# A fused attention and feed-forward kernel: its first two groups become two chunks of one batch each, with two neighbouring tokens per partition, and the order of the program is written anew

## The chip, the core and the metric

The kernel runs on one core of a Trainium2 chip. The metric is device time in microseconds (us); the median of three runs of the kernel before is 174.61 us (174.01 to 174.85). The core's engines are named as the profile names them: PE (matrix products; PEld is its load of weights), DVE, ACT and POOL (element-wise work), SP (it only issues DMAs here).

## The reference

Four batches of 768 tokens, 8 heads of 48. First a linear attention with a decaying state per head, then a feed-forward block on all 3072 tokens:

```
for t in range(S):
    cur = einsum('bhd,bhe->bhde', u * kt, vt)
    y[:, :, t] = einsum('bhd,bhde->bhe', rt, state + cur)
    state = w * state + einsum('bhd,bhe->bhde', kt, vt)
h = x @ w_in                 # x: y as [3072, 384]; w_in [384, 2048]
g = where(h >= 1, h, where(h <= -1, 0, (h + 1)**2 / 4))
out = g @ w_out              # w_out [2048, 384]
```

## The kernel before

Tokens are cut into chunks of 128. A unit is one chunk of one batch; a **group** is two units, worked on together, and there are 12 groups. Group g covers chunk g // 2 of the batches 0 and 1 (g even) or 2 and 3 (g odd). So the groups 0 and 1 hold chunk 0 of all four batches, and no state enters them. Units are numbered n = 2g + j.

Within a chunk the recurrence is done as matrix products. The names of the steps are those of the word list `ORDER`, each of which calls the function `do_<name>`:

- `ln`, `bw`, `bu`, `wq`: the logarithm of w, laid over all partitions by a float32 matmul with a row of ones (tile lwp, L207), the same for u (tile up, L211), and per column (tile wp, L233). `WupS`, `WdnS`, `Wup`, `Wdn` make from lwp the tables of powers of w, on ACT.
- `LR`, `LK`, `LV`: DMA loads of r, k and v (tiles Ri, Ki, Vi), issued on SP's queue. In the groups 0 and 1 each is in two halves, one for each unit, of 192 KB; a piece of memory that lies together is one token of one head, 48 floats or 192 bytes.
- `Rs`, `Ks`: r and k times the tables, to bfloat16. `TR`, `TK` turn them by PE, `cR`, `cK` copy them out of PSUM (tile TT). Later groups are turned by DMA (`RT`, `KT`).
- `A`: products of k and r of the chunk (L370, eight matmuls for a unit, 48 rows of weights each). `AT`: the causal mask on DVE (L384; 128x512 here, two for a unit).
- `KU`, `RKU`, `us`, `B`: the part of the token itself, u k r v. `V`: cast of v (ACT).
- `Y` (L432, L438): A times v, and r times the state from the second chunk on. `y`: sum with B, on DVE.
- `X`, `xc`: y turned by PE and copied; later groups by a DMA transpose, `xcg` (L467).
- `Sp`, `Tm`, `decay`, `sbf`: the new state.
- `m` (L475): one of four blocks of h of a group, 12 matmuls. `r`, `s`, `g` make the activation from it: L486 and L495 on ACT, L498 on DVE. `M` (L512): a quarter of the second product for one unit, four matmuls, one for each f. `og`, `stg`: copy and store.
- `Z`: matmuls on a tile of zeros, with which PE fills waiting time.

The recording is by hand: every engine runs its own instructions in the order of `ORDER`, and a program waits only where data, a buffer or a PSUM bank asks for it. The letter behind `=` names the engine, the digits behind `/` PSUM banks or pairs of banks; while the groups 0 and 1 are in their attention part some banks are used singly (`bank`), else in four pairs (`pair`), which m, M, T, A, Y, Sp and X share. A step that asks for a pair waits until the pair's last reader is through. The weights w_in and w_out come by three DMAs each from POOL's queue (`WI`, `WO`), which cast to bfloat16; the third of either has the blocks 2 and 3.

Of the kernel before, what the change touches and what calls it, by code (L numbers as in the profile page):

```python
# [25 lines left out]
TK0/0 Wup/1 Rs0.0=V TR0/3 LK1.1 cK0=A WupS KU0.1=G KU0.0=V RKU0.0=G cR0=A KU1.0=G LV0.1 Rs0.1=V Z2 TR1/1 A0/03 LV1.0
LV1.1 WI0 WI1 WI2 us0.0 cR1=A TK1/1 cK1=A AT0.1 Z4 A1/13 Rs1.0=V LR2.0 LR2.1 Rs1.1=V V0.1 AT1.0 V0.0 Z9 TR3/1 B0.0=G
AT1.1 RKU0.1=V wE AT0.0 wC=A us0.1 Z7 Y1/3 TR2/0 B0.1=G Y0/2 y0 y1 cR2=A RKU1.0=G Z8 X0/2 Z4 TK2/3 X1/0 Ks1.1=G xc0=A
Sp1/2 cK2=A xc1=A Z7 TK3/3 cK3=A Tm1 A2/20 m0.0/0 cR3=V us1.0 AT2.1 AT2.0 r0.0=A A3/31 AT3.1 KU1.1=G RKU1.1=G m0.1/1
V1.0 s0.0=A B1.0=G Sp2/2 AT3.0 us1.1 r0.1=A Tm2 Y2/3 y2 g0.0 V1.1 X2/0 LK2.0 Y3/1 B1.1=G s0.1=A LK2.1 Sp0/2 Sp3/3  # L30
xc2=V LK3 y3 WO0 WO1 m0.3/0 r0.3=A s0.3=A g0.1 X3/1 Tm0 xc3=V m0.2/1 LR3 LV2.0 Tm3 m1.1/2 g0.3 r1.1=V m1.0/3 m1.2/0
Ks2=G r0.2=A s0.2=A g0.2 sbf2=A s1.1=A r1.0=A s1.0=A sbf3=A g1.1 m1.3/1 r1.2=V WO2 KU2=G LV2.1 M0.00/2 M0.10 M0.11
M0.01 g1.0 M1.00/3 M1.10 M1.11 M1.01 Rs2=G s1.2=A g1.2 T5/0 RKU2=G LK4 r1.3=A s1.3=A g1.3 T4/1 LV3 Ks3=G M0.02 M0.03
LR4 us2 c5=V A5/0 KU3=G Rs3=G c4=V A4/1 AT5 sbf1=A M1.02 M0.12 M0.13 AT4 T6/0 sbf0=A V2 Y4/1 Y5 B2=G og0=A T7/2 c6=A
# [40 lines left out]
def kernel(  # L75
# [52 lines left out]
    nc.scalar.dma_start(out=u_row, in_=u.rearrange("(o h) d -> o (h d)", o=1))
# [5 lines left out]
    nc.vector.memset(idle, 0.0)
# [78 lines left out]
    def do_Wup(e, b):  # L213
        t = tiles["up_t"] = pair(b[0], F32, "up_t")[:, 0, :DM]
        nc.scalar.activation(t, flat(tiles["lwp"]), AF.Exp, scale=up_col)

    def do_Wdn(e, b):
        t = tiles["dn_t"] = bank(b[0], [P, DM], F32, "dn_t")
        nc.scalar.activation(t, flat(tiles["lwp"]), AF.Exp, scale=dn_col)
# [391 lines left out]
```

## Time and profile before

| | us |
|---|---|
| median of three runs | 174.61 |
| span of the profiled execution | 172.6 |
| PE busy | 164.4 |
| DVE busy | 130.6 |
| ACT busy | 129.9 |
| POOL busy | 117.4 |

The profile gives the span of its one execution, from the first to the last instruction; 2.0 us lie between it and the median of the timed runs. The span falls into a start, in which the groups 0 and 1 go through attention and PE waits and fills (up to about 27 us), a long middle in which PE is busy without a break but for a short one near 74 us, and an end of some 3 us after PE's last matmul. In the timeline's rows the numbers are start and length, then engine, line, operation, output<-input, form and count; a bracket tells how long the engine had been idle before and what ended that.

### The profile page before, as it was taken

Reading aid. Unit: us, or ns where it says so; the run is one execution under the profiler, and the core shown is the slowest. Engines: PE = TensorE matmul, PEld = TensorE weight load, DVE = VectorE, ACT = ScalarE, POOL = GpSimd, SP = SyncE. Lnnn points to the kernel's source line nnn. Section 1 sums busy time; section 2 is a strip of 40 time slices with the busy share of each in tenths; the row PEclk is TensorE's granted clock in tenths of the full one; section 3 lists DMA queues with packets and bytes.
Section 4 is the critical chain, followed back from the end, with each engine's and each line's share of the span. In section 5 each row is a group of like instructions: output and inputs, shape, how many; then the busy total and the mean of one; then the engine's idle time right before and its main releaser. Section 6 shows DMA issues by size and latency. Waiting matters only on the chain.

```text
span 172.6 us, 4051 instructions
## 1 busy us (share of the span) xinstructions
PE 164.4 (95%) x1674; PEld 132.9 (77%) x1674; DVE 130.6 (76%) x150; ACT 129.9 (75%) x150; POOL 117.4 (68%) x86
## 2 busy tenths in 40 slices
PE   7989968999999999989999999999999999999991
PEld 5769868966889777588787797696897787888871
DVE  4578698988687688859789779885889959873752
ACT  4355698991699899189979879689695896988940
POOL 3496744998689949999999998999568804300000
PEclk9999999999999999999999999999999999999999
DMA  6999999998996999999999997998999025140022
GB/s 114 194 184 179 199 187 180 228 210 174 206 191 99 206 184 168 194 199 145 196 312 210 182 220 163 223 182 155 297 170 267 4 52 145 37 104 0 8 91 91
DMA packets 103751, 28.26 MB, mean 164 GB/s; under 512 B 98866, under 2 KB 102836, under 8 KB 103732
## 3 DMA queue, kind: packets, MB, share of 16 engines
q1 hardware_dynamic: 101824, 24.75, 79.9%
q0 software_dynamic: 1760, 3.15, 9.8%
q8 instruction: 13, 0.21, 0.6%
q10 hardware_dynamic: 148, 0.10, 0.2%
q14 instruction: 6, 0.05, 0.1%
HBM read 20.45 MB, written 4.72 MB: 146 GB/s over the span
## 4 chain that ended last, share of the span: by engine, by line
PE 87%; ACT 4%; DMA 2%; DVE 2%; issue 1%; POOL 0%; ACTq 0%; DVEq 0%
PE hp L475 35%; PE op L512 34%; PE A L370 4%; PE Y L438 3%; DMA xT<-y 2%; PE Y L432 2%; PE Sp L405 2%; PE z L566 2%; ACT pt L486 1%; PE T L330 1%; ACT TT L112 1%; PE lwp L207 1%; PE wp L233 1%; PE TR L330 1%; PE TK L330 1%
## 5 line engine op out<-in xcount | busy, mean ns | idle before, releaser
L475 PE MATMUL hp<-xT,w_in 128*128 128x256 bf16 x576 | 69.1, 273 | 1.3 <-DMA xT<-y 0.8
L512 PE MATMUL op<-w_out,g 128*128 128x384 bf16 (+1 forms) x400 | 68.4, 320 | 0.0
L498 DVE SCALAR_TENSOR_TENSOR g<-sq,hp 128x1024 bf16<-128x1024 bf16 x48 | 57.9, 1215 | 13.2 <-ACT sq L495 13.2
L475 PEld LDWEIGHTS <-w_in 128*128 128x128 bf16 x576 | 61.9, 114 | 4.6 <-issue 1.6
L486 ACT ACTIVATE pt<-hp 128x1024 f32<-128x1024 f32 x46 | 46.9, 1021 | 13.7 <-PE hp L475 13.7
L512 PEld LDWEIGHTS <-g 128*128 128x128 bf16 x400 | 37.5, 98 | 20.4
L495 ACT ACTIVATE sq<-pt 128x1024 bf16<-128x1024 f32 x46 | 48.3, 1057 | 1.2
L379 DVE TENSOR_TENSOR AT<-A,umask 128x1024 bf16<-128x1024 f32 x20 | 23.7, 1220 | 5.2 <-PE A L370 5.2
L282 POOL TENSOR_TENSOR Ks<-Ki,Wdn 128x768 bf16<-128x768 f32 (+1 forms) x12 | 20.3, 1689 | 8.5 <-ACT Wdn L225 3.4
L313 POOL TENSOR_TENSOR V<-Vb,diag 128x768 f32<-128x768 bf16 (+1 forms) x14 | 18.1, 1291 | 9.8 <-DVE diag L304 4.4
L282 POOL TENSOR_TENSOR RKU<-Ri,KU 128x768 f32<-128x768 f32 (+1 forms) x13 | 21.2, 1630 | 1.1 <-DVE KU L282 0.7
L282 POOL TENSOR_TENSOR KU<-Ki,u_sb 128x768 f32<-128x768 f32 (+1 forms) x13 | 21.2, 1634 | 0.4 <-DMA Ki<-in_k_dram 0.4
L416 POOL TENSOR_TENSOR state<-Tm,wCm 128x768 f32<-128x768 f32 x8 | 14.6, 1824 | 9.8 <-DVE Tm L413 9.8
L282 POOL TENSOR_TENSOR Rs<-Ri,Wup 128x768 bf16<-128x768 f32 x10 | 18.2, 1820 | 0.3 <-DMA Ri<-in_r_dram 0.3
L112 ACT CAST Vb<-Vi 128x768 bf16<-128x768 f32 (+1 forms) x14 | 10.2, 733 | 5.4 <-DMA Vi<-in_v_dram 5.4
L450 DVE TENSOR_TENSOR y<-Y,V 128x768 bf16<-128x768 f32 x10 | 9.6, 956 | 5.9 <-PE Y L438 3.3
L304 DVE TENSOR_REDUCE diag<-RKU 128x16 f32<-128x768 f32 (+1 forms) x14 | 11.6, 831 | 1.5 <-POOL RKU L282 1.5
L112 ACT CAST state_bf<-state 128x768 bf16<-128x768 f32 (+1 forms) x12 | 8.5, 717 | 4.4 <-POOL state L416 4.4
L112 ACT COPY o<-op 128x768 f32<-128x768 f32 (+1 forms) x9 | 6.7, 748 | 6.0 <-PE op L512 5.9
L438 PE MATMUL Y<-Vb,AT 128*128 128x48 bf16 x192 | 10.4, 186 | 0.4 <-ACT Vb L112 0.4
L438 PEld LDWEIGHTS <-AT 128*128 128x128 bf16 x192 | 9.5, 98 | 0.7 <-issue 0.5
L413 DVE TENSOR_TENSOR Tm<-Sp,state 128x768 f32<-128x768 f32 x8 | 7.7, 956 | 3.1 <-PE Sp L405 3.1
(73 smaller groups left out, 123.3 us busy)
## 6 DMA issues: line engine op xcount, KB each, us to landing
out_dram<-o SPq DMA_DIRECT2D x11, 384.0 KB, 3.8
Ki<-in_k_dram SPq DMA_DIRECT2D x9, 384.0 KB, 6.2
Ri<-in_r_dram SPq DMA_DIRECT2D x9, 384.0 KB, 6.2
Vi<-in_v_dram SPq DMA_DIRECT2D x9, 384.0 KB, 5.4
Ki<-in_k_dram SPq DMA_DIRECT2D x6, 192.0 KB, 4.0
Ri<-in_r_dram SPq DMA_DIRECT2D x6, 192.0 KB, 4.7
Vi<-in_v_dram SPq DMA_DIRECT2D x6, 192.0 KB, 6.0
w_in<-in_moe_w_in_dram POOLq DMA_DIRECT2D x2, 384.0 KB, 7.5
```

The costliest lines, as they stand in the source:

```text
L112: nc.scalar.copy(out, in_) if e == "A" else engines[e].tensor_copy(out, in_)
L282: engines[e].tensor_mul(part(out)[:, :, :, :D], part(a), rep(b, j1 - j0) if len(b.shape) == 3 and b.shape[1] == H else part(b))
L304: nc.vector.tensor_reduce(d[:, hs], tiles["RKU", g][:, hs, :], AX.X, ALU.add)
L313: engines[e].tensor_mul(t[:, hs, :], tiles["V", g][:, hs, :], tiles["diag", g][:, hs].unsqueeze(2).to_broadcast([P, n, D]))
L379: nc.vector.tensor_mul(t.rearrange("p i n t -> p (i n) t"), tiles["A", n].rearrange("p i (n t) -> p (i n) t", t=P), umask.unsqueeze(1).to_ ...
L416: engines[e].tensor_mul(states[g % BP], tiles["Tm", g], flat(wCm).unsqueeze(1).to_broadcast([P, UNITS, DM]))
L438: nc.tensor.matmul(Y[:, h * D : (h + 1) * D], AT[:, i, p, :], V[:, j * H + h, :], start=(c == 0), stop=True, skip_group_check=True,)
L475: nc.tensor.matmul(hp[:, f, :], w_in_sb[wi][:, i, wo * FG * P + f : (wo + 1) * FG * P : FG], tiles["xT", g][:, :, i, :], start=(i == 0), s ...
L486: nc.scalar.activation(t, tiles["hp", g, q], AF.Relu, bias=0.5, scale=0.5)
L495: nc.scalar.activation(t, p, AF.Square)
L498: nc.vector.scalar_tensor_tensor(out=make("g", ("g", g, q), [P, FG, TOK], BF16), in0=tiles["sq", g, q], scalar=1.0, in1=tiles["hp", g, q], ...
L512: nc.tensor.matmul(tiles[key][:, i, : o1 - o0], tiles["g", g, q][:, f, j * P : (j + 1) * P], w_out_sb[wi][:, wo, f * DO + o0 : f * DO + o1 ...
```

## The change

- **Groups.** Group 0 is chunk 0 and chunk 1 of batch 0, group 1 the same of batch 1 (`place`). The groups 2 and 3 take chunk 0 and chunk 1 of the batches 2 and 3. From group 4 on all is as it was.
- **Two tokens per partition.** In the groups 0 and 1 partition q holds the tokens 2q and 2q + 1 of the 256. A load of r, k or v for the group is one DMA of 384 KB over all partitions, with 384 bytes lying together. The two "units" of such a group are now the even and the odd tokens, `e`. Partitions 0 to 63 are chunk 0, 64 to 127 chunk 1.
- **Products in quarters of the array.** `A` does 16 matmuls for a unit in place of 8, with 48 rows and 64 columns of weights and 128 moving columns (L431). `Y` does 32 in place of 8, with 64 rows, 64 columns of weights and 48 moving columns (L513 and the lines around it), and `Ys` four more that add the state of chunk 0 to the second half. `Sp` does 8 in place of 4, from 64 rows each. The mask becomes one for each parity (`pmask`). Chunk 0's state must be there before chunk 1's `Ys`, within the group.
- **Tables.** ACT makes four tables (`U`, `D`, for even and odd tokens) into two PSUM pairs before the first copies, and `WupS`, `WdnS` later.
- **Full-height float32 matmuls.** ones, u_row and lnw have 128 partitions, of which all but the first of the latter two are zero, so the float32 matmuls of `bw`, `bu` and `wq` run over 128 rows, not one. u_row's DMA waits for a memset.
- **Weights.** The third part of w_in (`WI2`) is loaded first, and the blocks m0.2 and m0.3 come before m0.0 and m0.1; the third part of w_out first too.
- **End.** The two halves of the last unit's output lie in PSUM pairs of their own, and both are stored from SP's queue; before, one was issued by ACT.
- **Order.** `ORDER` is new up to m4.0, with some element-wise steps on other engines (RKU1.0, RKU2, B1.1, B2 and B3 on DVE, V0.0 on POOL); behind m4.0 it is the same sequence with other PSUM pairs. Buffers: g 12 for 13, TT 2 for 3, and two of the new tile TG.

```
-Zs/0 ln Z19 bw/1 LK0.0 bu/0 uS=V LK1.0 LR0.0 LK0.1 LR0.1 LV0.0 wq/2 WdnS Ks1.0=G LR1.0 LR1.1 Wdn/3 Ks0.0=V Ks0.1=V
...
+Z17/0 bu/3 LR0 ln=A LK0 uS=V bw/2 U1=A/1 Rs0.1=V D1=A/0 Ks0.1=V U0=A KU0.1=G wq/0 Rs0.0=V D0=A wE=A TR1/3 cR1=A
...
+    def place(g):
+        return (0, 0) if g < JOINT else (g - JOINT, 1) if g < 2 * JOINT else divmod(g, BP)
...
-    u_row = const.tile([1, DM], F32, name="u_row")
+    u_row = pool.tile([P, DM], F32, name="u_row", tag="pt", bufs=SLOTS["pt"])
...
+    nc.vector.memset(u_row, 0.0)
+    nc.scalar.dma_start(out=u_row[:1], in_=u.rearrange("(o h) d -> o (h d)", o=1))
...
-    ones = const.tile([1, P], F32, name="ones")
+    ones = const.tile([P, P], F32, name="ones")
...
+    def do_U(e, b, i):
+        table(b, "up2", i, up2_col[i])
+
+    def do_D(e, b, i):
+        table(b, "dn2", i, dn2_col[i])
...
+        if g < JOINT:
+            nc.sync.dma_start(
+                out=t.rearrange("p (h e) d -> p h (e d)", e=2),
+                in_=x[g, :, : UNITS * C, :].rearrange("h (q e) d -> q h (e d)", e=2),
+            )
+            return
...
+                for j in range(UNITS):
+                    half = slice(j * HP, (j + 1) * HP)
+                    nc.tensor.matmul(
+                        A[i][half, p, :], by_parity(n)[rows, NP + p, half], tiles["TG", n // UNITS][rows, :, p, half],
+                        start=True, stop=True, skip_group_check=True,
+                    )
...
+                        nc.tensor.matmul(
+                            Y[rows, h * D : (h + 1) * D], tiles["AT", UNITS * g + i][rows, h % 2, h // 2, j * HP : (j + 1) * HP], tiles["V", g][rows, i * H + h, :],
+                            start=(h == 0 and i == 0), stop=(i == 1 and b == 0), skip_group_check=True,
+                        )
...
+    def do_Ys(e, b, n):
+        g = n // UNITS
+        for p in range(NP):
+            cols = slice(2 * p * D, 2 * (p + 1) * D)
+            nc.tensor.matmul(tiles["Y", n][HP:, cols], by_parity(n)[:, p, HP:], states_bf[0][0][:, g, cols], start=False, stop=True, skip_group_check=True)
...
-        key = ("op", g, j) if last else ("op", g)
...
+            key = ("op", g, j, i) if last else ("op", g)
...
-stA11.1=A oB11.1=V stB11.1
+oA11.1=A stA11.1 oB11.1=V stB11.1
```

Three places show what the new order does. The first is PE's order behind the first run of `z` matmuls, before:

```order
L207 MATMUL lwp<-lnw,ones 128x384
L211 MATMUL up<-u_row,ones 128x384
L233 MATMUL wp<-ones,lnw 128x1 x4
L330 LDWEIGHTS Ks
L330 MATMUL TK<-ident,Ks 128x128
```

and now:

```order
L236 MATMUL up<-u_row,ones 128x384
L232 MATMUL lwp<-lnw,ones 128x384
L261 MATMUL wp<-ones,lnw 128x1 x4
L382 LDWEIGHTS Rs
L382 MATMUL TR<-ident,Rs 128x128
```

The matmul for u now stands ahead of the one for lwp, from which all the tables are made, and r is turned before k. The second place is DVE's order from the first group's masks to its y and the first copy of x, before (A's number tells the PSUM tile; V_278 is group 0's product B):

```order
L304 TENSOR_REDUCE diag<-RKU 128x8
L384 TENSOR_TENSOR AT<-A_213,umask 128x512
L282 TENSOR_TENSOR Rs<-Ri,Wup 128x8x48 x2
L384 TENSOR_TENSOR AT<-A_244,umask 128x512
L384 TENSOR_TENSOR AT<-A_245,umask 128x512
L282 TENSOR_TENSOR RKU<-Ri,KU 128x384
L384 TENSOR_TENSOR AT<-A_212,umask 128x512
L304 TENSOR_REDUCE diag<-RKU 128x8
L446 TENSOR_TENSOR y<-Y,V_278 128x384 x2
```

and now:

```order
L356 TENSOR_REDUCE diag<-RKU 128x8
L326 TENSOR_TENSOR Rs<-Ri,up_181 128x8x48
L332 TENSOR_TENSOR Ks<-Ki,dn_184 128x8x48
L448 TENSOR_TENSOR AT<-A_258,pmask_127 128x512
L448 TENSOR_TENSOR AT<-A_259,pmask_127 128x512
L448 TENSOR_TENSOR AT<-A_294,pmask_131 128x512
L448 TENSOR_TENSOR AT<-A_295,pmask_131 128x512
L480 TENSOR_TENSOR state<-Sp,wCm 128x384
L356 TENSOR_REDUCE diag<-RKU 128x8
L483 TENSOR_TENSOR Tm<-Sp,state 128x384
L542 TENSOR_TENSOR y<-Y,V_436 128x384 x2
```

Group 1's Rs and Ks now stand ahead of the four masks, and two steps of the new state behind them, before y. The third place is DVE's order from group 1's masks to group 2's, now (V_542 is group 1's product B, made here on DVE):

```order
L448 TENSOR_TENSOR AT<-A_546,pmask_127 128x512
L594 SCALAR_TENSOR_TENSOR g<-sq,hp 128x1024
L542 TENSOR_TENSOR y<-Y,V_542 128x384
L594 SCALAR_TENSOR_TENSOR g<-sq,hp 128x1024
L365 TENSOR_TENSOR V_542<-Vb,diag 128x384
L542 TENSOR_TENSOR y<-Y,V_542 128x384
L115 COPY xT<-X 128x384
L443 TENSOR_TENSOR AT<-A,umask 128x1024
L115 COPY TT<-T 128x1024
L594 SCALAR_TENSOR_TENSOR g<-sq,hp 128x1024
L443 TENSOR_TENSOR AT<-A,umask 128x1024
L322 TENSOR_TENSOR RKU<-Ri,KU 128x768
```

where before stood:

```order
L384 TENSOR_TENSOR AT<-A_406,umask 128x512
L304 TENSOR_REDUCE diag<-RKU 128x8
L409 TENSOR_TENSOR state<-Sp,wCm 128x384
L446 TENSOR_TENSOR y<-Y,V_437 128x384
L498 SCALAR_TENSOR_TENSOR g<-sq,hp 128x1024
L112 COPY xT<-X 128x384
L446 TENSOR_TENSOR y<-Y,V_437 128x384
L498 SCALAR_TENSOR_TENSOR g<-sq,hp 128x1024
L409 TENSOR_TENSOR state<-Sp,wCm 128x384
L112 COPY xT<-X 128x384
```

Group 2's masks, the copy of its turned tiles and a product of POOL's now stand among the first `g` steps; before, they came after all eight `g` of the groups 0 and 1.

More of the change, by code (lines that the diff above doesn't have):

```diff
@@ L24 @@
 ORDER = """
-Zs/0 ln Z19 bw/1 LK0.0 bu/0 uS=V LK1.0 LR0.0 LK0.1 LR0.1 LV0.0 wq/2 WdnS Ks1.0=G LR1.0 LR1.1 Wdn/3 Ks0.0=V Ks0.1=V
[L26 to L34, printed above, removed]
@@ new lines @@
+KU0.0=G TK1/1 LR1 LK1 Ks0.0=V TR0/0 TK0/3 WdnS=A cR0=A RKU0.1=G cK0=A WI2 Rs1.1=V LV0 Ks1.1=V us0.1=V Z19/0 A0/03
+Rs1.0=V Ks1.0=V V0.0=G KU1.1=G AT0.0=V AT0.1=V cK1=A WupS=A Zp6/1 A1/21 V0.1=A wC=A AT1.0=V TK3/0 LV1 cK3=A LR2.1
+RKU0.0=G Zp3/0 Sp0/3 AT1.1=V TR3/2 Sp1/0 Tm0=V us0.0=V Tm1=V Y1/1 cR3=A sbf0=A V1.1=A V1.0=A Y0/3 Ys1 B0.1=G RKU1.1=G
+y1=V TK2/2 Ys0 Sp2/0 B0.0=G KU1.0=G y0=V cK2=A X1/1 decay1=G X0/2 LK2.1 LR2.0 LK2.0 WI0 xc1=A Tm2=V Sp3/3 xc0=V
+us1.1=V TR2/1 Tm3=V RKU1.0=V us1.0=V sbf2=A m0.2/1 cR2=A r0.2=A LK3 WI1 A3/10 s0.2=A B1.0=G Rs2=G Ks2=G A2/32 AT3.1=V
@@ L211, in do_bu, with table @@
         nc.tensor.matmul(t, ones, u_row, start=True, stop=True)
[L213 to L219, printed above, removed]
+    def table(b, what, i, col):
+        if what not in tiles:
+            tiles[what] = pair(b[0], F32, what)
+        nc.scalar.activation(tiles[what][:, i, :DM], flat(tiles["lwp"]), AF.Exp, scale=col)
+    def do_U(e, b, i):
+        table(b, "up2", i, up2_col[i])
+    def do_D(e, b, i):
+        table(b, "dn2", i, dn2_col[i])
     def do_WupS(e, b):
@@ L369, in do_A @@
                 rows = slice(i * HP, i * HP + D)
-                nc.tensor.matmul(A[i][:, p, :], turned(n, 1, p)[rows], turned(n, 0, p)[rows], start=True, stop=True)
+                if n >= UNITS * JOINT:
+                    nc.tensor.matmul(A[i][:, p, :], turned(n, 1, p)[rows], turned(n, 0, p)[rows], start=True, stop=True)
+                    continue
+                for j in range(UNITS):
[4 more added lines that the diff above has]
+                    )
     def do_AA(e, b, g):
@@ L403, in do_Sp @@
         for p in range(NP):
+            if g < JOINT:
+                rows = slice(j * HP, (j + 1) * HP)
+                for i in range(2):
+                    h = i * H + 2 * p
+                    nc.tensor.matmul(Sp[:, p, :], flat(tiles["Ks", g][rows, h : h + 2, :]), flat(tiles["V", g][rows, h : h + 2, :]), start=(i == 0), stop=(i == 1))
+                continue
             h = j * H + 2 * p
```

194 lines of the change are left out of this document (126 added, 68 removed).

## The prediction

> **What bounds the kernel now.** I read the page first, then the stretches, then the chain of waits.
>
> ```profile
> span 172.6 us, 4051 instructions
> PE 87%; ACT 4%; DMA 2%; DVE 2%; issue 1%; POOL 0%; ACTq 0%; DVEq 0%
> 20.00:30.00 10.00, 8.15 (x99) 7.44 (x98) 8.96 (x15) 8.02 (x10) 4.31 (x6) 1.00 1.00 186
> 30.00:40.00 10.00, 10.00 (x86) 7.83 (x84) 9.19 (x10) 8.58 (x11) 9.98 (x7) 1.00 1.12 216
> ```
>
> PE holds 87% of the chain. In the stretches (PE, PEld, DVE, ACT, POOL, then the clock column, DMA share and GB/s) PE stops being the bound only ahead of 30 us: 8.15 of 10 us, with DVE at 8.96. Behind that it is full. So the change can win or lose in three places: the start, short gaps of PE, the end. The chain shows them:
>
> ```profile
> 3.44 1.64 PE lwp L207 x2
> 5.09 1.28 PE up L211 x2
> 10.82 0.60 PE TK L330 x4
> 12.69 1.07 PE z L566 x9
> 17.27 0.22 PE z L566 x4
> 17.49 0.22 PE TK L330 x4
> 19.28 1.45 PE hp L475 x12
> 27.27 6.73 PE hp L475 x60
> 39.20 0.89 PE T L330 x16
> 41.39 0.55 PE A L370 x16
> 45.64 0.65 PE op L512 x4
> 68.81 0.96 DVE y L450
> 69.80 4.27 DMA xT<-y
> 74.11 1.47 PE hp L475 x12
> ```
>
> PE's first useful block m0.0 starts at 19.28, and the eighth block of the groups 0 and 1 ends at 27.27 + 6.73 = 34.0. These two moments are my marks. Ahead of 17 us PE runs at half rate: nine z took 1.07 us (119 ns each), and four took 0.22 (55 ns) at 17.27; turning took 0.60 at 10.82 and 0.22 at 17.49. The clock column shows 1.00 throughout, so here the durations tell the clock, not the column. At 68.81 the chain leaves PE once: y, its DMA transpose, and 74.11.
>
> **The start, step by step.** These rows carry the times:
>
> ```profile
> 0.99 2.21 PE L566 MATMUL z<-idle 128*128 128x128 bf16 x19 [0.99 <-DVE idle L134]
> 1.12 0.48 DVE L138 MEMSET lnw<- 1x512 f32 x1
> 1.31 0.23 ACTq L128 DMA_DIRECT2D u_row<-in_u_dram  x1
> 5.12 0.58 ACT L225 ACTIVATE Wdn<-lwp,dn_col 128x384 f32<-128x384 f32 x1 [1.73 <-PE lwp L207]
> 6.07 0.56 ACT L215 ACTIVATE up_t<-lwp,up_col 128x384 f32<-128x384 f32 x1
> 7.18 1.00 POOL L282 TENSOR_TENSOR KU<-Ki,u_sb 128x384 f32<-128x384 f32 x1 [0.40 <-DMA Ki<-in_k_dram]
> 12.73 1.29 DVE L384 TENSOR_TENSOR AT<-A,umask 128x512 bf16<-128x512 f32 x2 [0.37 <-PE A L370]
> 13.35 0.92 ACT L112 CAST Vb<-Vi 128x384 bf16<-128x384 f32 x2 [1.32 <-DMA Vi<-in_v_dram]
> 14.73 0.53 PE L438 MATMUL Y<-Vb,AT 128*128 128x48 bf16 x8
> 16.15 1.02 DVE L446 TENSOR_TENSOR y<-Y,V 128x384 bf16<-128x384 f32 x2 [0.61 <-PE Y L438]
> L112 ACT COPY TT<-TK 128x512 bf16<-128x512 bf16 x4 | 2.3, 586 | 2.6 <-PE TK L330 2.5
> L282 DVE TENSOR_TENSOR Rs<-Ri,up_t 128x384 bf16<-128x384 f32 x2 | 1.1, 544 | 0.0
> L498 DVE SCALAR_TENSOR_TENSOR g<-sq,hp 128x1024 bf16<-128x1024 bf16 x48 | 57.9, 1215 | 13.2 <-ACT sq L495 13.2
> L379 DVE TENSOR_TENSOR AT<-A,umask 128x1024 bf16<-128x1024 f32 x20 | 23.7, 1220 | 5.2 <-PE A L370 5.2
> ```
>
> *Tables.* up now stands ahead of lwp. z ends two matmuls sooner (3.20 - 2 x 0.12 = 2.96), up adds 1.28, so lwp starts at 4.24 and not at 3.44: a loss of 0.8. The new wait is on ACT: u_row's DMA, and the table load and ln behind it, wait for a memset of 384 columns. At the rate of lnw's (512 in 0.48) that is 0.36, begun where ones and lnw are cleared now, and over near 1.31, where the DMA is issued today: I put it at nothing, with 0.2 if it is late. The first table comes at 5.12 + 0.8 = 5.9. ACT's exponentials follow at 0.475 (the first starts at 5.12, the third at 6.07). Four of them, w's column (0.2) and then the copies cR1, cR0, cK0 and the table Wdn between them (4 x 0.58) end at 5.9 + 1.9 + 0.2 + 2.3 = 10.3.
>
> *Filling.* Z19 waits for cR0 (9.7), and A0 is queued behind it on PE. At 55 ns it ends at 10.75 and costs 0.45 beyond cK0; at 107 it would end at 11.7.
>
> *The quarters.* No row shows a matmul on a quarter of the array. Nearest is A: 16 in 0.55, 34 ns each, with 48-row operands. If four quarters ran at once it could be half of that; with the array slow, Y's 8 in 0.53 give 66 ns. I take 34: A0 0.55, and Y1 with Y0, 64 matmuls, 2.2. A0 ends at 11.3.
>
> The Trainium skill's page "TensorEngine Tiling (Array Packing)" speaks against this change in its section "Tiling Modes": a switch of the tiling mode drains the array, and the section "Restrictions and Gotchas" adds that column tiling excludes the fast load of weights. No run here shows that yet; the rival on the quarters prices it.
>
> *Loads.* K0.1 is the fourth half load and ends a wait at 7.18; V0.1, the tenth, ends one at 13.35: 1.03 per 192 KB, which the stretch confirms as 193 GB/s. For runs of 1536 bytes the last stretch gives 62 GB/s at a share of 0.18, or 344.
>
> ```profile
> 2.50:13.30 10.80, 9.84 (x64) 7.07 (x63) 5.85 (x13) 5.09 (x10) 6.36 (x7) 1.00 1.36 193
> 160.00:173.00 13.00, 9.10 (x80) 7.31 (x77) 6.48 (x7) 5.97 (x7) 0.00 (x0) 1.00 0.18 62
> ```
>
> 384-byte runs lie between 193 and 344; I take 250, nearer to the lower, or 1.57 per 384 KB. Counting back four halves from 7.18, the data begin at 3.06. K1, the fourth, lands at 9.35 (at the old rate 11.3; at 344, 7.6), V0 at 10.9, V1 at 12.5. Behind K1 stand on DVE Ks1.1, us0.1, Rs1.0 and Ks1.0 (4 x 0.545): 11.5. So loads and A0 end together, and the first mask starts at 11.5.
>
> *Masks to m.* Four masks at 0.65 end at 14.1. Y1 and Y0 end at 16.3, Ys1 (four matmuls) at 16.45. Tm0, us0.0 and Tm1 lie beside Y on DVE. With 0.25 of delay as ahead of today's y, y1 and y0 (1.02) end at 17.7, Tm2 (0.55) and the copy of x (0.35) at 18.6. m0.2 starts at 18.7, 0.6 sooner than today's m0.0. WI2 is issued at about 9.5 on POOL, ahead of V0.0's cast; today it is the third of three.
>
> ```profile
> w_in<-in_moe_w_in_dram POOLq DMA_DIRECT2D x2, 384.0 KB, 7.5
> w_in<-in_moe_w_in_dram POOLq DMA_DIRECT2D x1, 768.0 KB, 12.6
> ```
>
> It took 12.6 behind the other two, a single one 7.5. Estimated between these it lands at 17 to 22: 18.7 covers it on average, and at the late end m0.2 would lose up to 3 us, of which DVE's queue hides most, since the masks of group 1 don't need it.
>
> *DVE's run to the eighth block.* From here DVE is the bound, as it is today in 20 to 30 us. Four short steps (2.2), four masks (2.6), g0.2 (1.2), y2 (0.55), g0.3 (1.2), B1.1 and y3 (1.1) end at 27.5. X3 waits for m0.0, whose pair is free at 26.4: the copy of x ends at 28.5. Then AT4, c5, g0.0, AT5, RKU2 and g0.1 (1.2 + 0.65 + 1.2 + 1.2 + 0.95 + 1.2 = 6.4) end at 34.9. m1.2 waits for g0.1's pair, and ends at 36.25, not 34.0: +2.25. But PE has by then done T4, T5 (0.89) and A4, A5 (0.55), which today follow later, and group 2 has no state to add (some 0.3): 1.75 given back. Net for the start: +0.5.
>
> **Gap and end.**
>
> ```profile
> 169.06 0.34 SPq L555 DMA_DIRECT2D out_dram<-o  x1
> 169.49 0.38 ACTq L539 DMA_DIRECT2D out_dram<-o  x1
> 169.87 0.34 SPq L539 DMA_DIRECT2D out_dram<-o  x1
> ```
>
> Between Y9 and m4.0 there are now seven M and not six: 0.65 (4 matmuls) more cover for the transpose that ends at 74.07: -0.65. At the end the second half need no longer wait for the first's copy, but its store now stands third on SP (169.06 + 3 x 0.34 = 170.08, not 170.21): -0.13. The moved steps on POOL cost nothing: it was never last in the chain (0%), and has fewer of them. SP issues the loads of the groups 2 and 3 in another order; only POOL's products wait for them, so that order is covered too. g at 12 buffers and TT at 2 I cost at nothing: the extra buffers cover reuse by much older groups; without that cover a g would wait for one M (0.65).
>
> Sum: +0.5 - 0.65 - 0.13 = -0.3. The span becomes 172.3; with the 2.0 that lie between this span and the median, **174.3**. A measurement of this kernel can tell about 0.5%, 0.9 us, from no change.
>
> **The rivals.**
>
> *The start gains more.* Loads at 344 (K1 at 7.6), full clock during lwp (0.64 less), quarters two at a time (Y1 and Y0 1.1 for 2.2): m0.2 at 16.9, and DVE's run, the bound behind it, 1.8 sooner: 172.5. For it: 2.0 of Z19 and the single-row matmuls are lost today. Against: WI2 must land by 17.
>
> *Quarters one after the other (slower).* If a quarter's weights hide behind nothing, each matmul costs 66 ns or more, up to the 98 ns of a weight load:
>
> ```profile
> L438 PEld LDWEIGHTS <-AT 128*128 128x128 bf16 x192 | 9.5, 98 | 0.7 <-issue 0.5
> ```
>
> At 66, Y1 and Y0 take 2.1 more, Y2 and Y3 one more beyond g0.2 and g0.3: 174.3 + 3.1 = 177.4; at 98, 181. It decides against the kernel from about 45 ns. By the Trainium skill's rule above it would go so, or nearly.
>
> *The clock stays slow (slower).* Single-row matmuls from 3.44 to 6.37 did not open it; a dense run from 12.6 to 17 did. If 128 rows of zeros do no better, Z19 costs 1.0 more, Y 2.1 more: 177.4. The Trainium skill's page "TensorE: Matmul & The Clock Gate", section "Part 1: The HAM clock gate (the "warmup" mystery)", asks for some 3.4 us of sustained work, on a window that does not start with the kernel. With that rule, z, up and lwp (0.99 to 5.9) should open it; the trace agrees on 12.6 to 17, but not on 0.99 to 6.37, where PE was as busy.
>
> *Loads no faster (slower).* K1 at 11.3 puts the first mask at 13.5: +2.0, 176.3.
>
> **Chances.** Forecast 0.40, its own range 173.3 to 175.2 (0.12 of it faster, 0.26 same, 0.02 slower). More gain 0.30, faster. Quarters one after the other 0.13, slow clock 0.10, loads 0.07: slower. So faster 0.42, same 0.26, slower 0.32. The range runs from 171.9, a little beyond the gain, to 177.2, short of the two dearest cases: left out are half of the quarters' and of the clock's chance and a little of the gain.
>
> **What would show it.** Right: z at 55 ns in Z19; a quarter's matmul near 34 ns in A and Y; first mask near 11.5, m0.2 near 18.7, the eighth block's end near 36 with T4, T5, A4, A5 ahead of it; DVE nearly full from 18 to 35; no wait ahead of m4.0. Wrong: PE's Y taking over 1.5 us each, turning still at 0.60 behind 8 us, a mask that waits for Ki, m0.2 waiting for w_in, or new gaps of PE behind 40 us, where I put none: the banks are dealt anew there, and a wait of one pair for its reader is 1 us.

## The result, and the profile after

The change made the kernel slower: a ratio of 1.0636 to the kernel before, 95% interval 1.0583 to 1.0688, in its first timing, and 1.0843 (1.0805 to 1.0882) in a repeat, with a median of 188.96 us. These two timings of one kernel lie 2% apart, which is more than their intervals, so a difference of that size between two versions of it carries little. Forecast were 174.3, and 177.2 as the upper end of the range. The ratios leave out every execution that took over 1.5% longer than the fastest of its kernel (seven of the twelve of the last run below), and as the first profile fell on such a one, of 425.1 us, in which PE was held back throughout, the profile shown here is of the repeat.

The page's span and chain, and in a second piece the stretches that answer to those of before (PE, PEld, DVE, ACT, POOL, then the clock column, DMA share and GB/s):

```profile
span 186.6 us, 4364 instructions
...
PE 73%; DVE 15%; ACT 5%; DMA 4%; issue 2%; DVEq 0%
```

```profile
20.00:30.00 10.00, 8.55 (x171) 7.51 (x169) 9.85 (x12) 7.27 (x10) 9.38 (x9) 1.00 1.21 201
30.00:40.00 10.00, 0.83 (x11) 0.58 (x11) 9.30 (x3) 0.96 (x1) 8.03 (x6) 0.68 1.15 212
40.00:50.00 10.00, 10.00 (x84) 8.41 (x81) 8.43 (x9) 6.13 (x7) 5.50 (x3) 0.81 1.05 168
```

The stretch from 30 to 40 is where the time went. PE worked 0.83 of its 10 us; before it was full there. DVE was "busy" for 9.30 with three instructions, and the clock column falls to 0.68 and 0.81. The chain of waits names the instruction:

```profile
20.27 1.31 PE hp L571 x12
...
21.98 2.48 DVE AT L448 x4
24.46 1.09 DVE g L594
25.60 0.56 DVE y L542
26.16 1.13 DVE g L594
27.29 11.18 DVE V L365
38.55 0.57 DVE y L542
39.17 0.50 PE X L556 x3
39.67 0.54 PE A L427 x8
40.21 0.96 PE T L382 x8
41.17 2.56 PE hp L571 x12
43.74 0.37 PE A L427 x8
44.11 5.49 PE hp L571 x48
```

L365 is step B1.1, the product of v and the diagonal for the second unit of group 1, which the change moved from POOL to DVE. The eighth block of h ends at 44.11 + 5.49 = 49.6; before it was 34.0. Behind these marks lie 186.6 - 49.6 = 137.0 us now and 138.6 before, so the whole loss and more is ahead of the mark. The timeline of DVE and of POOL around it:

```profile
27.20 11.25 DVE L365 TENSOR_TENSOR V<-Vb,diag 128x384 f32<-128x384 bf16 x1
38.55 0.56 DVE L542 TENSOR_TENSOR y<-Y,V 128x384 bf16<-128x384 f32 x1
...
24.60 1.81 POOL L322 TENSOR_TENSOR Ks<-Ki,Wdn 128x768 bf16<-128x768 f32 x1
26.37 1.86 POOL L275 DMA_DIRECT2D w_out<-in_moe_w_out_dram  x3
28.24 1.82 POOL L322 TENSOR_TENSOR KU<-Ki,u_sb 128x768 f32<-128x768 f32 x1
30.01 1.01 POOL L486 TENSOR_TENSOR state<-Tm,wCm 128x384 f32<-128x384 f32 x1
30.96 1.80 POOL L322 TENSOR_TENSOR KU<-Ki,u_sb 128x768 f32<-128x768 f32 x1
32.72 1.80 POOL L322 TENSOR_TENSOR Ks<-Ki,Wdn 128x768 bf16<-128x768 f32 x1
34.48 1.79 POOL L322 TENSOR_TENSOR Rs<-Ri,Wup 128x768 bf16<-128x768 f32 x1
36.24 1.79 POOL L322 TENSOR_TENSOR RKU<-Ri,KU 128x768 f32<-128x768 f32 x1
```

POOL runs six products without a pause, each starting as the one ahead of it ends, until 36.24 + 1.79 = 38.03. DVE's product ends at 27.20 + 11.25 = 38.45, 0.42 later. All that is queued behind it on DVE (y3, the masks of group 2, four g) waits, and PE for them: its idle time ahead of X is 10.36 us. PE then works at half rate for a while: its first block takes 2.56 for 1.31.

### The profile page after: what moved, and what is told of

Read it like the earlier page. It is cut to its first block, busy times and chain, and to the rows that moved or that the text cites. A ratio compares the mean times of both kernels' runs of the same rounds, so it can differ in the third digit from the quotient of the medians.

```text
span 423.3 us, 4364 instructions
## 1 busy us (share of the span) xinstructions
PE 418.3 (99%) x1827; PEld 235.1 (56%) x1827; DVE 143.1 (34%) x167; ACT 131.9 (31%) x149; POOL 111.7 (26%) x85
## 4 chain that ended last, share of the span: by engine, by line
PE 98%; DVE 1%; ACT 0%; issue 0%; DVEq 0%
PE hp L571 41%; PE op L608 40%; PE A L427 3%; PE Y L528 2%; PE Sp L475 2%; PE Y L522 2%; PE z L661 2%; PE Y L514 1%; PE T L382 1%; PE Sp L472 1%; PE X L556 1%; PE A L431 1%; PE TR L382 1%; PE wp L261 0%; PE up L236 0%; PE TK L382 0%
## 5 line engine op out<-in xcount | busy, mean ns | idle before, releaser
L571 PE MATMUL hp<-xT,w_in 128*128 128x256 bf16 x576 | 178.9, 535 | 0.0
L608 PE MATMUL op<-w_out,g 128*128 128x384 bf16 (+1 forms) x400 | 177.2, 665 | 0.0
L571 PEld LDWEIGHTS <-w_in 128*128 128x128 bf16 x576 | 101.8, 179 | 71.9 <-issue 14.1
L608 PEld LDWEIGHTS <-g 128*128 128x128 bf16 x400 | 68.1, 174 | 87.8 <-issue 80.7
L365 POOL TENSOR_TENSOR V<-Vb,diag 128x768 f32<-128x768 bf16 (+1 forms) x11 | 14.3, 1299 | 132.4 <-DVE diag L356 112.4
L322 POOL TENSOR_TENSOR Ks<-Ki,Wdn 128x768 bf16<-128x768 f32 x10 | 18.1, 1812 | 41.6 <-PE Sp L475 41.6
L546 DVE TENSOR_TENSOR y<-Y,V 128x768 bf16<-128x768 f32 x10 | 9.6, 956 | 45.7 <-issue 27.8
L322 POOL TENSOR_TENSOR RKU<-Ri,KU 128x768 f32<-128x768 f32 x9 | 16.3, 1807 | 20.4 <-DVE diag L356 20.1
L528 PE MATMUL Y<-Vb,AT 128*128 128x48 bf16 x160 | 18.9, 267 | 0.0
L322 POOL TENSOR_TENSOR KU<-Ki,u_sb 128x768 f32<-128x768 f32 x10 | 18.3, 1831 | 0.1
L528 PEld LDWEIGHTS <-AT 128*128 128x128 bf16 x160 | 16.4, 145 | 2.2 <-issue 1.0
L522 PE MATMUL Y<-state_bf,RT 128*128 128x96 bf16 x64 | 15.1, 305 | 0.0
```

The source lines that it names most:

```text
L322: engines[e].tensor_mul(part(out)[:, :, :, :D], part(a), rep(b, j1 - j0) if len(b.shape) == 3 and b.shape[1] == H else part(b))
L365: engines[e].tensor_mul(t[:, hs, :], tiles["V", g][:, hs, :], tiles["diag", g][:, hs].unsqueeze(2).to_broadcast([P, n, D]))
L522: nc.tensor.matmul(Y[:, 2 * p * D : 2 * (p + 1) * D], turned(n, 0, p), states_bf[bp][(c - 1) % 2][:, j, 2 * p * D : 2 * (p + 1) * D], star ...
L528: nc.tensor.matmul(Y[:, h * D : (h + 1) * D], AT[:, i, p, :], V[:, j * H + h, :], start=(c == 0), stop=True, skip_group_check=True,)
L571: nc.tensor.matmul(hp[:, f, :], w_in_sb[wi][:, i, wo * FG * P + f : (wo + 1) * FG * P : FG], tiles["xT", g][:, :, i, :], start=(i == 0), s ...
L608: nc.tensor.matmul(tiles[key][:, i, : o1 - o0], tiles["g", g, q][:, f, j * P : (j + 1) * P], w_out_sb[wi][:, wo, f * DO + o0 : f * DO + o1 ...
```

## The experiments

All times are against the kernel before on the same chip (medians 174.1 to 174.4).

**The change again, the float32 matmuls, the quarters.** The first four runs test the rivals of the prediction, as theories A (the clock), B (the start) and C (the quarters).

> The changed kernel, unchanged, for a trace with the clock mostly granted: the profiled execution above had PE held back from its first matmul to its last. Theory A (the clock is withdrawn for some microseconds within the run, as the clock shares of 0.98 and 0.93 of the other executions say): about 185 us, and PE's blocks of 12 matmuls take 1.31 us in most of the run but over 2 us in one stretch of 5 to 8 us. Theory B (the start is longer because up waits for u_row's DMA and the chain behind it is late): about 185 us with all blocks at 1.31 us once the first has run, and the eighth block of the groups 0 and 1 ending at about 45 us instead of 34. Theory C (matmuls on quarters of the array run one after the other): Y1 and Y0 at over 2 us each.

Measured: ratio 1.0843, and the trace shown above. Theory A's half clock is there (33.6 to 43.8), but behind PE's idle stretch; that it is a consequence shows further on, where it goes when the stalls go. Theory B's late eighth block is there (49.6), but u_row's share of it is small: PE waited 1.3 us for it. Theory C fails: Y1 and Y0 together, 64 matmuls, hold the chain for 1.12 us.

```
-        nc.tensor.matmul(t, ones, lnw[:, :, :D], start=True, stop=True)
+        nc.tensor.matmul(t, ones[:1], lnw[:1, :, :D], start=True, stop=True)
...
-        nc.tensor.matmul(t, ones, u_row, start=True, stop=True)
+        nc.tensor.matmul(t, ones[:1], u_row[:1], start=True, stop=True)
```

> The changed kernel with its float32 matmuls (up, lwp, wp) back on one row. Theory A, if the full height is what opens the clock early: the clock opens later, near 15 to 20 us, and the time rises by 1 to 3 us against the changed kernel. If the full height instead is what brings the withdrawal: the time falls by 5 to 10 us. Theory B: no change beyond 1 us, since up still waits for u_row. Theory C: no change.

Measured: 1.0529 (1.0494 to 1.0564), the eighth block at 49.9, and B1.1 again 11.25 us, in the profiled execution of 188.69 us; the half clock is there too, from 31.0 to 44.7. So the full height of the float32 matmuls brings neither the stall nor the loss of the clock behind it. Whether it costs time beyond that is open: the ratio is lower than that of the change, but the executions of this kernel took 183.1 to 190.0, and those of the change, but for the one of 425.1, 184.9 to 192.0. In the kernel before the reverse edit:

```
-    u_row = const.tile([1, DM], F32, name="u_row")
+    u_row = const.tile([P, DM], F32, name="u_row")
...
-    ones = const.tile([1, P], F32, name="ones")
+    ones = const.tile([P, P], F32, name="ones")
...
-    lnw = const.tile([1, H, HP], F32, name="lnw")
+    lnw = const.tile([P, H, HP], F32, name="lnw")
```

> The kernel before with its three float32 matmuls over 128 rows, nothing else changed. Theory A with the full height as the cause of withdrawals: some executions at 180 us and above with a clock share under 0.99. Otherwise: within 1.5 us of the kernel before, faster by up to 1 us if the clock then opens ahead of 10 us.

Measured: 0.9986 (0.9958 to 1.0015): nothing that can be told in the time. The trace does show something: the clock opened at 4.9 us, was lost again from 8.3 to 15.2 and then stayed, where in the kernel before it opened at 17.1. So 128 rows opened it early here, but not for good. The next one does A, Y, Ys and Sp with whole rows and columns of the array in place of quarters and halves:

```
-                for j in range(UNITS):
-                    half = slice(j * HP, (j + 1) * HP)
...
+                nc.tensor.matmul(A[i][:, p, :], by_parity(n)[rows, NP + p, :], tiles["TG", n // UNITS][rows, :, p, :HP], start=True, stop=True, skip_group_check=True)
```

> The changed kernel with every product of the groups 0 and 1 on quarters or halves of the array done on the whole of it: A 8 matmuls for a unit in place of 16, Y 16 in place of 32, Sp over 128 rows. It leaves out the products between the two parities of A and adds terms to Y and Sp that don't belong there. Theory C: faster by 4 to 8 us than the changed kernel. Theory A with the quarters as the cause (the tiling mode or its pauses let the clock go): about 174 us, clock share 1.0. Theory B: within 1 us of the changed kernel.

Measured: 1.0825 (1.0752 to 1.0898), no faster than the change, with B1.1 at 11.5 us in its profile. The quarters are not the cause.

**Who holds DVE up.** Theory S is read from the trace of the change: POOL's run and DVE's product end together. The next four runs are on one chip.

```
-B1.1=V m0.0/0 y3=V
+B1.1=G m0.0/0 y3=V
```

> The changed kernel with the one step B1.1 (values times the diagonal, group 1, second unit) given back to POOL, where it stands between two of POOL's w_out issues. Theory S (shared access): a DVE product with both inputs in SBUF is not served while POOL works without a pause; B1.1 took 11.25 us on DVE for that reason alone, and the clock was withdrawn because PE then stood idle. Expected: B1.1 takes 0.83 us on POOL, y3 starts before 30, the record of 0.5 clock at 33.56 to 43.8 is gone, and the time falls from 188.96 by 10 to 13 us, to 176-179. Theory O (other): the start and the order cost most of the 14 us, and B1.1 only stands where something else is late; then the time stays above 182.

Measured: 1.0464 (1.0441 to 1.0487), median 182.68: 6.3 us won against the change's 188.96. That is less than theory S had (10 to 13), and the time lies just where theory O had it (above 182), so by the time alone theory S is not shown here. B1.1 took 0.84 on POOL, and the trace shows why more was not won: the stall moved to the next DVE product of this kind, RKU2 (DVE, then POOL, in the profiled execution of 186.65 us):

```profile
37.40 1.22 DVE L443 TENSOR_TENSOR AT<-A,umask 128x1024 bf16<-128x1024 f32 x1
38.53 4.54 DVE L322 TENSOR_TENSOR RKU<-Ri,KU 128x768 f32<-128x768 f32 x1
43.00 2.34 DVE L594 SCALAR_TENSOR_TENSOR g<-sq,hp 128x1024 bf16<-128x1024 bf16 x2
...
38.67 1.82 POOL L322 TENSOR_TENSOR Rs<-Ri,Wup 128x768 bf16<-128x768 f32 x1
40.45 1.80 POOL L322 TENSOR_TENSOR RKU<-Ri,KU 128x768 f32<-128x768 f32 x1
43.16 1.81 POOL L322 TENSOR_TENSOR KU<-Ki,u_sb 128x768 f32<-128x768 f32 x1 [0.91 <-DMA Ki<-in_k_dram]
```

It ended at 43.07, 0.82 after POOL's run (42.25), which stopped for a load. In the next kernel all five moved products (B1.1, B2, B3, RKU1.0, RKU2) go back to POOL:

> The changed kernel with all five moved products with both inputs in SBUF (B1.1, B2, B3, RKU1.0, RKU2) given back to POOL. Theory S: against the kernel with B1.1 alone on POOL it wins what B2 (2.36 instead of 0.95) and RKU2 (1.64) lose on the path, 0 to 2 us, so 175-178, unless POOL, with 5 to 6 us of added work between 22 and 60, becomes late: then 0 to 3 us slower than it. Theory O: above 182 as well.

Measured: 1.0418 (1.0376 to 1.0461), median 182.31, level with the run ahead of it (the intervals overlap), and again above theory O's 182. No DVE instruction is held up, but now POOL is late, which the second branch of the expectation named: PE waits 4.1 us for y2, which waits for B2, which stands on POOL behind Rs5, which waits for its load until 47.17. So in this kernel a wait for POOL's order stands in place of the stall, and the two runs together do not yet decide between theories S and O.

The next leaves DVE's work as the change has it and makes POOL wait once:

```
+    def do_hold(e, b):
+        nc.gpsimd.tensor_copy(const.tile([1, 1], F32, name="held"), tiles["V2", 1][:1, UNITS * H - 1, :1])
...
-WO0 WO1 KU2=G decay3=G
+WO0 WO1 hold KU2=G decay3=G
```

> The changed kernel with B1.1 left on DVE, and one POOL copy of a single element of B1.1's result put behind the w_out issues and ahead of POOL's run KU2, state, KU3, Ks3, Rs3, RKU3, so that this run begins only after B1.1 has ended. Theory S: B1.1 takes 0.55 to 2 us (2 if POOL's issuing of the transfers holds DVE up as well, until 28.2), POOL's run begins at 28.2-29.3 and the time is 176-179. Theory D (the w_out transfers or their issue stall DVE): B1.1 stays above 4 us, since the issues still stand ahead of it. Theory F (the form, bf16 with a broadcast operand, is slow on DVE): B1.1 stays at about 11 us, the time at or above 188.

Measured: one run of 174.67 and three of 180.97 to 182.69. In the profiled one, of 182.69:

```profile
26.90 0.55 DVE L365 TENSOR_TENSOR V<-Vb,diag 128x384 f32<-128x384 bf16 x1
...
33.04 5.72 DVE L322 TENSOR_TENSOR RKU<-Ri,KU 128x768 f32<-128x768 f32 x1
...
26.05 1.86 POOL L275 DMA_DIRECT2D w_out<-in_moe_w_out_dram  x3
27.90 0.18 POOL L614 COPY held<-V 1x1 f32<-1x1 f32 x1
```

B1.1 takes 0.55, and that while POOL issues the w_out transfers. So neither the form (theory F) nor the issues (theory D) hold it up; what POOL does next does. RKU2 then takes the stall over: 5.72. The run of 174.67 left no trace, so what made it faster is not shown.

In the next, B1.1 stays on DVE as eight instructions with one tensor input each:

```
+            for h in range(hs.start, hs.stop):
+                nc.vector.tensor_scalar(t[:, h, :], tiles["V", g][:, h, :], tiles["diag", g][:, h : h + 1], None, ALU.mult)
```

> The changed kernel with B1.1 left on DVE at its place, but written as eight instructions that each multiply one head's 48 columns by a per-partition scalar, so that each has one tensor input. Theory S, in the form that only two tensor inputs in SBUF are held up: eight times 0.1 to 0.15 us, B1.1 done within 1.5 us, time 176-179. If any DVE instruction that reads SBUF alone is held up by POOL's run: the eight end after POOL's run, at about 38, and the time stays at 187-191.

Measured: 1.0608 (1.0585 to 1.0632). The eight took 8.45 together, from 26.88; the first alone 7.37, to 34.25, and POOL's run paused at 34.20. The rest took 0.23 each. So the narrow form of theory S falls: an instruction that reads v and a scalar per partition from SBUF is held up as well. Whether the scalar or the form does it, no run here tells.

**Taking the stalls away.** Here POOL waits twice, for B1.1 and for RKU2:

```
-WO0 WO1 KU2=G decay3=G g0.0=V AT5=V m1.3/1 m1.0/0 KU3=G Ks3=G RKU2=V
+WO0 WO1 hold1 KU2=G decay3=G g0.0=V AT5=V m1.3/1 m1.0/0 KU3=G RKU2=V hold2 Ks3=G
```

> The changed kernel with DVE's work as the change has it, and POOL made to wait twice by a copy of one element: ahead of KU2 for B1.1's result, and ahead of Ks3 for RKU2's. Theory S (a DVE product with both inputs in SBUF is served only when POOL's gapless run ends): with one wait RKU2 took the stall over (5.72 us against Ks3, Rs3, RKU3); with two, B1.1 takes 0.55 and RKU2 0.95, PE has no idle stretch over 2 us between 28 and 45, the clock's half-speed record there is gone, and the time is 173.5-176, as in the one of the runs with one wait that took 174.67. Theory R (rest): the start, the loads or the order cost the other 7 us; then 179-182 again, with RKU2 at 0.95.

Measured: 1.0149 (1.0108 to 1.019), median 177.0; B1.1 0.55, RKU2 0.95. Its stretches:

```profile
30.00:40.00 10.00, 10.00 (x94) 8.59 (x91) 9.56 (x10) 9.41 (x11) 8.54 (x7) 1.00 1.13 213
40.00:50.00 10.00, 9.82 (x109) 6.95 (x108) 9.58 (x10) 5.92 (x8) 7.42 (x5) 1.00 1.16 172
```

PE is full and the clock whole: with no work taken from DVE, 12 of the 14.7 us are gone. The time lies 1.0 above the range of theory S and 2.0 below that of theory R. So the two stalls, with the clock lost behind them, are most of what the change lost; this is the run that shows it. The eighth block ends at 37.4. Two products still wait, for one POOL instruction each, and both stand in the chain (DVE, then POOL):

```profile
42.82 2.27 DVE L365 TENSOR_TENSOR V<-Vb,diag 128x768 f32<-128x768 bf16 x1
51.23 2.07 DVE L365 TENSOR_TENSOR V<-Vb,diag 128x768 f32<-128x768 bf16 x1
...
42.46 1.81 POOL L322 TENSOR_TENSOR KU<-Ki,u_sb 128x768 f32<-128x768 f32 x1 [2.26 <-DMA Ki<-in_k_dram]
44.23 2.53 POOL L322 TENSOR_TENSOR Ks<-Ki,Wdn 128x768 bf16<-128x768 f32 x1
```

B2 and B3 lose 1.3 and 1.1 over the 0.95 that such a product takes undisturbed; that is 2.4, most of the 2.7 between 177.0 and the forecast, if all of it reaches the end. Ks4 shows the other side: 2.53 in place of 1.81, since DVE got in first.

The next puts B1.1, RKU2 and B2 on POOL, but where POOL has time, and leaves B3 and RKU1.0 on DVE:

```
-B1.1=V
+B1.1=G
...
-KU2=G decay3=G
+KU2=G RKU2=G decay3=G
...
-KU4=G Ks4=G V2=A
+V2=A B2=G KU4=G Ks4=G
```

> The changed kernel with B1.1, RKU2 and B2 back on POOL, and RKU2 placed right behind KU2 and B2 ahead of KU4, so that y2 no longer waits for B2 behind Rs5, which waits for its load (47.1 in the kernel with all products on POOL). Theory S: no DVE instruction is held up for over 1 us before 60, PE has no idle stretch over 2 us between 28 and 52, time 173-177. Theory R: 179-182.

Measured: 1.0090 (1.0056 to 1.0125), median 176.33. No DVE instruction waits ahead of 50; then, against the expectation, B3 does: it takes 2.60 us from 50.28. With ln(w)'s product ahead of u's as well:

```
-Z17/0 bu/3 LR0 ln=A LK0 uS=V bw/2 U1=A/1
+Z17/0 LR0 ln=A LK0 bw/2 bu/3 uS=V U1=A/1
```

> The kernel before this one in the list with the ln(w) product ahead of the u product on PE, so that the tables do not wait for the landing of u_row. The step of the forecast that put this wait at nothing: no difference, within 0.3 us. If the wait is on the path, as the first table at 7.2 instead of 5.9 in the changed kernel suggests: 0.8 to 1.6 us faster than with u first.

Measured: 1.0000 (0.9972 to 1.0029), median 174.45: level with the kernel before. The first table starts at 5.18 for 6.89. But only part of the 1.9 us is the price of that wait: the eighth block ends just 0.3 earlier (36.7 for 37.0), and B3 now takes 1.04, not 2.60. The two are not told apart by these runs.

**The same stall in the kernel before.** One product moved to DVE beside a run of POOL:

```
-M0.01 g1.0
+M0.01 RKU2=V g1.0
...
-T5/0 RKU2=G LK4
+T5/0 LK4
```

> The kernel before with one edit: RKU2 moved from POOL to DVE, right ahead of g1.0, where it starts at about 34.7 beside POOL's run Rs2, Ks3, KU3, Rs3 (to about 40.3). Theory S: it takes 5 to 7 us instead of 0.95, the g products behind it are late, PE idles some us at 38-43, the time rises by 2 to 8 us, to 176-182. Theory F (something of the changed kernel alone, its layout or its order, made the product slow): 0.95 us, and the time stays within 0.7 of 174.3, since POOL wins 1.8 us and DVE has slack.

Measured: 1.0343 (1.0303 to 1.0384), with POOL's work 1.8 us less and DVE's 0.95 more. DVE, then POOL:

```profile
34.55 4.61 DVE L282 TENSOR_TENSOR RKU<-Ri,KU 128x768 f32<-128x768 f32 x1
39.09 3.47 DVE L498 SCALAR_TENSOR_TENSOR g<-sq,hp 128x1024 bf16<-128x1024 bf16 x3
...
34.78 1.80 POOL L282 TENSOR_TENSOR Ks<-Ki,Wdn 128x768 bf16<-128x768 f32 x1
36.55 1.79 POOL L282 TENSOR_TENSOR KU<-Ki,u_sb 128x768 f32<-128x768 f32 x1
39.56 1.80 POOL L282 TENSOR_TENSOR Rs<-Ri,Wup 128x768 bf16<-128x768 f32 x1 [1.22 <-DMA Ri<-in_r_dram]
```

The product takes 4.61, a little under the 5 to 7 expected, and ends at 39.16, 0.82 after POOL falls idle at 38.34 (here because Rs3 waits for a load). PE waits 3.9 us for g1.0, and a record of half clock follows, 38.9 to 45.7. So the layout and the order of the change are not needed for the stall: theory F falls.

**What is left at the start.** Two runs on the kernel with ln(w) first. In the first, uS stands behind Rs0.1 and Ks0.1 on DVE; in the second, Z19 is cut to 11 matmuls as well.

> The kernel with ln(w) first and the products back on POOL, with one more edit: DVE's copy of the u table (uS) behind Rs0.1 and Ks0.1 instead of ahead of them, since it waits for PE's u product until 6.4 and the third table waits 1.31 us for Rs0.1. If the path through the start is what sets the end in a kernel free of stalls, as ln(w) first suggests (start 1.7 earlier, end 1.9 earlier): the third table 0.6 to 0.9 earlier and the time 0.3 to 0.9 lower, 173.5-174.2. If PE's work, full from 10 us on, or the loads (group 1's K lands at 8.96) set the end: no difference within 0.3.

Measured: 1.0010 (0.9990 to 1.0029). The third table is 1.15 earlier (6.36 for 7.51), the eighth block 1.0 earlier (35.7), the time the same: here an earlier start no longer makes an earlier end.

> The kernel before this one in the list with Z19, the filler in front of the first A products, cut to 11 matmuls. If the filler holds the first A product back (it ends at 12.3, and what A waits for is there at about 11): 0.5 to 1 us faster. If the filler is needed for the clock to open: the clock opens 1 to 3 us later than at 14.2 and the time is 0.5 to 2 us slower.

Measured: 1.0009 (0.9983 to 1.0036): no difference. The clock opened at 11.2 in its profile and at 10.9 in the one ahead of it, so the eight matmuls taken away were not what opened it. No version of the change beat the kernel before.

## Why the prediction was wrong, point by point

**The step that failed** is "B1.1 and y3 (1.1)" in DVE's run to the eighth block. B1.1 was priced at 0.55, the duration of such a product with nothing beside it. It took 11.25, because it reads both inputs from SBUF while POOL works. The prediction looked at POOL's queue only for what the moved steps cost POOL ("it was never last in the chain"), never for what POOL's products cost DVE. The trace of before could not show it by itself: DVE's products with both inputs in SBUF lay where POOL did no element-wise work. For example (DVE, then POOL):

```profile
11.80 0.55 DVE L282 TENSOR_TENSOR Rs<-Ri,Wup 128x384 bf16<-128x384 f32 x1
13.93 0.55 DVE L282 TENSOR_TENSOR RKU<-Ri,KU 128x384 f32<-128x384 f32 x1
...
11.72 1.55 POOL L244 DMA_DIRECT2D w_in<-in_moe_w_in_dram  x2
14.36 0.82 POOL L313 TENSOR_TENSOR V<-Vb,diag 128x384 f32<-128x384 bf16 x1 [1.10 <-ACT w_col L236]
```

The steps on DVE beside POOL's run were g, AT, y and copies out of PSUM, all with an input in PSUM, and the reductions to the diagonal, with a single input in SBUF (0.95 at 39.05, beside POOL's KU); none was slow. The change has the same contrast within itself: the products Rs and Ks of its start, whose tables lie in PSUM, took their 0.55 beside POOL's products (DVE, then POOL):

```profile
11.28 0.55 DVE L326 TENSOR_TENSOR Rs<-Ri,up 128x384 bf16<-128x384 f32 x1
...
11.08 1.00 POOL L339 TENSOR_TENSOR KU<-Ki,u_sb 128x384 f32<-128x384 f32 x1
```

So the change moved products into a situation that the old order, by its choice of engines, never had. Of the five moved ones, three were held up in this trace (B1.1 with 11.25, RKU2 with 1.64, B2 with 2.36); RKU1.0, at 20.74 beside POOL's w_in issues, took 0.55, and B3 0.95. That it is the place of the inputs that decides is read from this contrast; no run moved one input of B1.1 to PSUM.

The Trainium skill's page "SBUF — State Buffer", section "Who interferes with whom", says that a DVE instruction with two SBUF inputs contends with a POOL (GpSimd) instruction that reads SBUF, that the shared ports are an exclusive lock, and that the order of issue decides which of the two waits. It would have named the rival. The runs agree on who contends. On the order of issue and the length of the wait they do not: by the recorded starts B1.1 came first (27.20, against 28.24 for KU), and it waited through six of POOL's instructions. The same section counts scalar products (`tensor_scalar`) among those that can contend, under conditions that no run here tests; the eight instructions that waited fit it.

The price in five places: the end of DVE's product against the end of POOL's run.

| run | product | alone | POOL's run ends | product ends | difference |
|---|---|---|---|---|---|
| the change | B1.1 | 0.55 | 38.03 | 38.45 | 0.42 |
| the change | RKU2 | 0.95 | 46.12 | 46.93 | 0.81 |
| B1.1 on POOL | RKU2 | 0.95 | 42.25 | 43.07 | 0.82 |
| POOL waits once | RKU2 | 0.95 | 37.94 | 38.76 | 0.82 |
| kernel before, RKU2 on DVE | RKU2 | 0.95 | 38.34 | 39.16 | 0.82 |

Each time the product does its work just after POOL has stopped. These are the waits that ended with a run of POOL; B2 and B3 got in earlier, as the last section says.

**The other steps.** The start of the change (ACT, DVE, PE):

```profile
7.18 0.56 ACT L241 ACTIVATE up<-lwp,up_col 128x384 f32<-128x384 f32 x1 [3.75 <-PE lwp L232]
13.65 2.48 DVE L448 TENSOR_TENSOR AT<-A,pmask 128x512 bf16<-128x512 f32 x4 [1.36 <-PE A L431]
4.24 1.62 PE L236 MATMUL up<-u_row,ones 128*128 128x384 f32 x2 [1.26 <-DMA u_row<-in_u_dram]
10.96 2.18 PE L661 MATMUL z<-idle 128*128 128x128 bf16 x19 [0.32 <-ACT TG L115]
16.34 1.19 PE L514 MATMUL Y<-Vb,AT 64*64 64x48 bf16 x64
```

- *Tables.* Lwp was to start at 4.24; up did, after 1.26 us of waiting for u_row. The memset ahead of u_row's DMA was rightly put at nothing (the DMA was issued at 1.37, for 1.31 before); the step left out is the DMA itself, which took 2.73 us in the chain and now has nothing ahead of up to cover it. The first table came at 7.18, not 5.9.
- *Filling and the clock.* The z of Z19 took 115 ns each, not 55, so A0 began at 13.2 (11.3 was its end by the forecast). The clock did open earlier than before, 13.1 for 17.1, but not by the height of the float32 matmuls, since with one row it opened at 14.0: the rival of the slow clock was half right, and its price was near 1 us (19 z at 115 ns for 55), not 3.
- *The quarters* were mis-sized the good way: in Y 1.12 / 64 = 17.5 ns each, not 34. With the whole array Y took 0.90 for 32, or 28 each, so quarters cost 0.22 more there. What the Trainium skill's page "TensorEngine Tiling (Array Packing)" says in "Tiling Modes" of draining at a switch of the mode can be no more than that cost in Y.
- *Loads.* Group 1's K landed at 9.05 (forecast 9.35) and its V at 12.13 (12.5), from the landings in the trace: right, and the rival on the loads falls.
- *Masks to m.* First mask 13.65 for 11.5; y1 and y0 end at 19.1 for 17.7; m0.2 at 20.3 for 18.7. WI2 landed at 17.4, inside its bounds, and no m waited for it.
- *Eighth block.* Forecast 36.25. With the two long stalls gone it was 37.4, and 36.7 with ln(w) first: this row of the sum was right to 0.5 to 1.2 us but for the stall.
- *Behind the eighth block* the forecast won 1.75 + 0.65 + 0.13 = 2.5. The kernel with ln(w) first has 172.6 - 36.7 = 135.9 there, the kernel before 138.6: 2.7 won. The total is right; the parts are not all. In the change itself the wait ahead of m4.0 stayed (0.7, PE for xT); it was 0.9 with POOL waiting twice, and gone with ln(w) first. The end gave nothing: 3.5 us from PE's last matmul to the end in both.

So a start some 2 us longer and as much won back, the balance that the forecast drew, does appear (1.0000), but not in the kernel that was forecast: that one has ln(w) first and three products back on POOL. The change as it was written, freed of its two long stalls alone, stood at 1.0149. The likeliest case failed on one wait that neither the sum nor a rival had.

## What to carry to other kernels

When a step moves from one engine to another, look up what the *other* engines do in the same microseconds and what they share: in these traces an element-wise product of DVE whose inputs both lie in SBUF waited while POOL ran its own, for one of POOL's instructions or until POOL paused (0.55 became 11.25). Price such a step by POOL's run beside it, not by its duration elsewhere. Give the product to POOL, put it where POOL waits anyway, or keep one input in PSUM (no run here made this last edit); and remember that an idle stretch of PE of about 4 us cost a second time here, by the clock.

## What the runs showed of the hardware beyond that

- *Idle PE loses the clock.* Behind 10.4 us of idle PE the half-rate record was 10.2 us long (33.6 to 43.8), behind 3.9 it was 6.8, behind 4.1 it was 3.4. Without such a stretch (POOL waiting twice, ln(w) first) there was none between the opening and PE's last products. A block of 12 matmuls costs 2.56 there, for 1.31. The Trainium skill's page "TensorE: Matmul & The Clock Gate", section "Part 1: The HAM clock gate (the "warmup" mystery)", speaks of an idle window of some 3.4 us; these three agree. It is not the only way to lose the clock: in the kernel before with 128 rows, with B1.1 on POOL and with POOL waiting once, it opened at 4.9 to 7.4 and was lost again 3.4 us later, for 3.4 to 17.1 us, with no idle stretch of PE over 0.9 us in between. What decided that is open.
- *When DVE gets in is open.* In four of the five rows above DVE's product passed one or more boundaries between POOL's products without its turn; B2 and B3 got in at the first boundary (POOL waiting twice), and POOL's product behind each took 2.53 and 2.56 for 1.81. And B1.1 began 1.0 us ahead of KU2, while POOL was only issuing transfers: in the change it did not get through, with POOL made to wait it did. The recorded starts of POOL may not be those at which it takes hold. No run settles this.
- *One tensor input is not always a protection.* The DVE product by a scalar per partition, all in SBUF, waited 7.1 us (7.37 for 0.23), while a reduction of one tensor in SBUF did not wait (0.95 at 39.05 in the kernel before).
